# Small scales in PSUM or off VectorE, attention's scale in the softmax, and a new written order

## The chip, the cores and the metric

The kernel runs on one core of a Trainium2 chip. The metric is the device time of one execution in microseconds (us). The engines of the core are called by the names of the profile: PE (TensorE, the matrix engine; PEld are its weight loads), DVE (VectorE), ACT (ScalarE), POOL (GpSimd) and SP (SyncE, which here only issues DMAs). SBUF is the on-chip memory, PSUM the small memory in eight banks that PE writes to. PE, DVE and ACT use PSUM; POOL works in SBUF.

## The reference

Three blocks in a row on a batch of 4, a sequence of 576 and a width of 512 (8 heads of 64):

```python
scores = q @ k.T / 8                       # causal mask, and a bias
bias = -(cum[:, None] - cum[None, :])      # cum: running sum of max(s, 0)
attn = softmax(scores + minimum(bias, 0))
x = attn @ v                               # attention, B x S x 512
h = relu(x.T @ w_tok1) @ w_tok2            # mixing over the sequence
u = x + h.T
y = u + relu(u @ w_ch1) @ w_ch2            # mixing over the channels
gate = sigmoid(conv5(y, conv_w))           # 5 causal taps per channel
out = (gate * (y @ w_val)) @ w_out
```

Inputs and outputs are float32 values; the weights arrive in 8 bytes each and are decoded in the kernel.

## The kernel before

[...] Before a split the operand is divided by a power of two near its largest magnitude, so that both halves fit in float16. These powers of two, and products and reciprocals of them, are the "small scales": tensors of 128 rows and 1 to 4 columns.

A scale over all rows is made by `over_partitions` (line 531): PE turns a column into a row, DVE takes the maximum and masks it to its exponent (`band`), PE spreads the result over 128 rows by a matmul with a piece of the identity (`unit`), and DVE applies a lower bound. `Pair.scales` does it for q, k and v of a pair of heads, `su_prep` for a batch's u, `Chunk.x_scale` for a chunk's y; `Weight.scale` makes a weight's scale from sums that lie in PSUM.

The work is tiled as follows. A batch has four pairs of heads (`Pair`); a pair has five row blocks for each head (`score`, `expo`, then `p_split` or `p_turn`, then `av`). The four pairs of batch 0 are "wide": their probabilities stay in float32 and are turned by PE, not split. `norm` takes the reciprocals of the softmax sums, `x_value` multiplies attention's result by them (into `x32`), `x_split` splits `x32` into `xn`, `x_turn` turns it for the residual `R`, `tok1` and `tok2` mix over the sequence, and `tok2_out` adds to `R`. Then two chunks per batch (`Chunk`, 320 and 256 positions) run `ch1`, `ch2`, the convolution, `val` and `outp`. The attention of the next batch runs beside the chunks of the current one.

In batch 0 there is nothing to run beside: while its attention runs, the weights are loaded, decoded (`decode`: shifts and ors on DVE, conversions on ACT), scaled and split. The first matmul of `ch1` of batch 0 needs all four pairs and `su_prep`.

The order of the instructions is a written table, `ORDER`: each entry names an engine (P, V, A, G, S) and a task's number, and each engine's queue runs in that order. Where a step may run on one of several engines (`one` for first halves, `two` for second halves), the table chooses. A planner (`Plan`) walks the table with cost formulas; the only thing that its estimates decide in the program is how many filler matmuls `keep_warm` puts before a PE step that is expected to come late (line 526: `ones` by `ones` into an unused part of a bank; they keep PE's clock up and compute nothing). Buffers come from pools of fixed depth; tag `B` stands for seven PSUM banks that all steps share, and `give("B")` marks the point from which a bank may be reused.

Every instruction that the planner records has line 256 in the profile, so tiles and shapes tell the steps apart. Names there: `xm` is the bank of `over_partitions`, `xg` its masked column, `gm` a pair's three scales, `sg` their reciprocals, `sc` constants for the scores, `sums` the softmax sums, `xbank` attention's result in PSUM, `raw`, `top` and `arena` the weights, `wsg` a weight's reciprocal scale, `su` and `sx` the scales of u and y.

Of the kernel before, what the change touches and what calls it, by code (L numbers as in the profile page):

```python
# [8 lines left out]
F32 = mybir.dt.float32  # L9
# [10 lines left out]
TINY = 2.0 ** -90  # L20
# [8 lines left out]
    one=1852.52, two=84.11, two_w=-7.7, taps=1388.05, sign=123.61, fill=-32.64, value=0, copy=0,  # L29
)  # L30

COSTS = dict(
    one=dict(A=(0.833, 186), V=(0.52, 1130), G=(0.84, 310)),
# [47 lines left out]
S12 S0 V0 S7 P8 P1 A13 V1 S10 V1 P1 A13 V13 V1 A11 V13 V1 A11 V11 V11 P13 S138 P11 A3 A9 S139 S21 S18 A2 V2 A3 A9 V9  # L81
V9 A2 V2 S2 G5 G5 A141 A141 A141 S32 P9 V14 V14 A17 G17 A16 S27 S140 V3 P142 V142 V142 P142 V142 V142 V142 V143 V143
A144 V144 S191 S30 P19 A22 A22 V16 S145 V22 V22 P28 A29 A29 V29 A20 P22 S34 S145 S190 G15 V15 V29 A31 A20 V20 V20
P20 G6 G6 A33 A33 V33 V33 P33 S46 V23 V23 A31 V31 S192 S41 G6 S242 V31 A35 A35 V35 G146 P169 V169 A170 P155 V155
A156 P149 V149 A150 P153 V153 A154 P147 V147 A148 P161 P175 V175 P178 V178 P171 P31 G25 G25 P29 A193 P151 V161 V171
A151 S44 A193 S48 P157 A157 P176 A193 V176 P179 V179 G24 P157 A157 A162 P159 A172 V159 A177 A160 V26 G6 P152 P152
P194 V194 V194 V35 P194 V194 V194 V194 V196 V195 V196 V195 S197 S197 G24 P42 P157 A157 A180 P173 A173 P35 V36 V36
S58 G39 V40 G40 A43 P158 P158 P163 A163 P173 A173 P163 A163 P181 A181 P173 P163 A163 P164 P164 V165 V165 V166 G167
A43 V43 A173 A45 A45 V45 V45 P181 A181 A47 A47 V47 V43 P181 A181 P174 P174 P182 P182 S243 P45 S69 A38 V167 P168 A49
A49 V49 A49 P43 S55 A168 V47 S244 V183 V183 V184 A185 G198 P199 P201 P207 V199 P221 P213 P211 P230 V201 P227 A200  # L90
V207 A202 P203 A203 A208 V213 A214 G49 P49 S60 P205 P47 S62 V185 P187 P187 V211 A212 P215 V227 P228 V205 P186 V221
P223 G4 V230 P231 A245 S294 A187 V187 P188 V50 V231 V228 P188 P56 A245 A186 A245 P246 G39 A215 V50 V246 V188 V246
P215 V223 A206 P209 P204 P246 V246 V189 A222 G51 V246 G53 P204 V246 V248 V247 V248 V247 S249 S249 G250 G54 G37 V189
V189 A215 A209 A59 P209 A209 A224 P209 A209 P215 A215 A59 A229 P225 A232 S296 P210 P210 P216 P216 V217 V217 V218
P233 V59 V59 A225 A57 P225 A233 P233 A225 P225 A233 A225 A57 V57 V57 P233 A233 P70 A71 A71 V71 A61 G37 P226 P226
P234 P234 S295 P220 P59 G219 V219 V71 P71 S72 P257 G38 A63 A63 V63 V235 G51 P253 A61 V61 A220 V235 A236 G237 V63
V257 A258 P265 V265 A266 V253 A254 P259 V259 A260 P251 V251 A252 P279 V279 P275 V275 P273 G54 V61 P282 A297 V237
P255 V282 A255 V273 S467 P63 P261 P256 P256 A297 A261 S74 A297 P263 P61 A73 A274 G52 P280 P57 V64 P298 V298 V298 S76
A276 A73 P261 V263 A264 A261 P283 P298 V298 V298 P239 S468 V298 A299 V280 A281 G300 V300 P267 A267 P277 A277 P239
P267 V299 S301 A75 V283 V64 G66 P261 A267 A261 P262 P262 P267 G52 P238 V73 V73 P73 S78 G53 S301 A75 V75 A284 P285  # L100
S469 V75 A239 V239 A267 P268 P268 A77 A77 V77 P277 A285 P285 P240 V269 V269 V270 V271 V271 A470 P240 V240 A77 A285
A277 P277 P285 P75 A238 V241 V241 V241 A277 P278 P278 A79 A79 V79 V79 A470 G77 G302 P311 V311 P305 V305 P309 V309
# [1660 lines left out]
```

## Time and profile before

| what | us |
|---|---|
| median of 3 timed runs | 648.89 |
| lowest and highest | 648.29, 650.25 |
| profiled execution, whole time | 648.36 |
| its span, first to last instruction | 646.2 |

In the span the engines are busy: PE 94%, PEld 76%, DVE 78%, ACT 59%, POOL 38%. The page's slices of 16 us show PE at two tenths in the first slice and seven in the second, and at nine or more in most slices from the third on; DVE stands at eight or nine tenths in most slices up to the thirty-first. The granted clock of PE is nine tenths or more in every slice. PE's busy time includes the filler matmuls, so the share alone says little on the early slices; they are read with line 526 taken off.

### The profile page before, as it was taken

The numbers are of one execution on the slowest core, as the hardware profiler recorded it, in microseconds if no ns is written. First come the engines' busy times: TensorE is split into PE (matmuls) and PEld (weight loads), VectorE is DVE, ScalarE is ACT, GpSimd is POOL, SyncE is SP. The second block draws the span as 40 slices with busy tenths as digits, with TensorE's granted clock in tenths as the row PEclk, the third lists the DMA queues.
The fourth block names the chain that finished last, engine by engine and source line by source line (L and its number), as shares of the span: only waits on it lengthen the run. The fifth ranks groups of instructions, "written<-read, shape, count | busy, mean of one in ns | idle before, by whom it ended". The sixth has DMA issues, their size and how long they took to land.

```text
span 646.2 us, 15964 instructions
## 1 busy us (share of the span) xinstructions
PE 609.8 (94%) x6092; PEld 491.5 (76%) x6092; DVE 502.5 (78%) x1394; ACT 380.5 (59%) x809; POOL 244.1 (38%) x343
## 2 busy tenths in 40 slices
PE   2799899979999999999999999998999999999997
PEld 2789798866788888677787787776878877678864
DVE  6898899899898988888879968886798752535772
ACT  5597798877767794546674575436676502123343
POOL 1544657352443434441443344454333310641100
PEclk9999999999999999999999999999999999999999
DMA  8988676687754858582756394835673300000012
GB/s 224 233 203 237 146 199 180 167 194 154 170 115 96 163 96 153 98 177 61 145 87 132 64 168 88 177 72 104 102 133 62 84 1 34 1 2 1 1 50 82
DMA packets 190807, 75.19 MB, mean 116 GB/s; under 512 B 178213, under 2 KB 181381, under 8 KB 190730
## 3 DMA queue, kind: packets, MB, share of 16 engines
q1 hardware_dynamic: 190730, 74.16, 53.2%
q8 instruction: 48, 0.79, 0.5%
q14 instruction: 29, 0.24, 0.1%
HBM read 33.89 MB, written 4.83 MB: 60 GB/s over the span
## 4 chain that ended last, share of the span: by engine, by line
PE 51%; DVE 6%; DMA 4%; issue 2%; SPq 1%; POOL 1%; ACT 1%; POOLq 0%; ACTq 0%; DVEq 0%
PE c L256 28%; PE v L256 7%; PE o L256 6%; PE t L256 3%; DMA pT<-p 3%; PE S L256 3%; PE xbank L256 3%; DVE gate L256 2%; DVE x L256 1%; SPq L256 1%; POOL p L256 1%; DMA qk<-qkT 1%; DVE p L256 1%; PE xT L256 1%; DVE R L256 1%
## 5 line engine op out<-in xcount | busy, mean ns | idle before, releaser
L256 PEld LDWEIGHTS <-arena 128*128 128x128 f16 x3168 | 287.7, 98 | 69.2 <-issue 2.8
L256 PE MATMUL c<-hT,arena 128*128 128x256 f16 (+1 forms) x1152 | 158.6, 286 | 0.0
L256 PE MATMUL c<-u,arena 128*128 128x256 f16 (+1 forms) x1152 | 156.2, 286 | 1.0 <-DVE hT L256 0.7
L256 ACT ACTIVATE x<-x,st 128x448 f32<-128x448 f32 (+4 forms) x160 | 85.0, 556 | 49.6 <-DVE st L256 48.7
L256 POOL TENSOR_TENSOR p<-x,p 128x320 f16<-128x320 f32 (+4 forms) x82 | 67.6, 829 | 114.1 <-ACT p L256 71.3
L256 DVE CUSTOM_DVE_ANT_0 x<-S,mask,sc 128x192 f32<-128x192 f32 (+4 forms) x160 | 73.7, 484 | 19.4 <-PE S L256 14.6
L256 ACT ACTIVATE hT<-c 128x320 f16<-128x320 f32 (+1 forms) x96 | 37.4, 405 | 78.7 <-PE c L256 77.5
L256 DVE SCALAR_TENSOR_TENSOR hT<-c,hT 128x320 f16<-128x320 f32 (+1 forms) x96 | 41.3, 448 | 34.4 <-ACT hT L256 34.3
L256 PE MATMUL xbank<-v,pT 128*128 128x65 f16 (+1 forms) x880 | 60.8, 208 | 3.2 <-DMA pT<-p 3.2
L256 DVE SCALAR_TENSOR_TENSOR gate<-R,cwt,gate 128x320 f32<-128x320 f32 (+1 forms) x104 | 57.0, 567 | 1.1
L256 PE MATMUL v<-x,arena 128*128 128x256 f16 (+1 forms) x384 | 53.2, 286 | 0.0
L256 PE MATMUL S<-qkT 128*128 128x64 f16 (+4 forms) x192 | 49.2, 277 | 3.5 <-DVE st L256 1.1
L256 PE MATMUL S<-qk 67*128 67x64 f16 (+4 forms) x192 | 49.7, 278 | 2.9 <-DMA qk<-qkT 2.8
L256 POOL TENSOR_SCALAR p<-x 128x192 f16<-128x192 f32 (+4 forms) x44 | 20.0, 456 | 72.5 <-ACT x L256 41.1
L256 PE MATMUL o<-arena,g 128*128 128x512 f16 x192 | 45.1, 379 | 0.0
L256 PEld LDWEIGHTS <-pT 128*128 128x128 f16 x960 | 37.3, 98 | 7.7 <-DMA pT<-p 3.9
L526 PE MATMUL xbank<-ones 128*128 128x112 bf16 x485 | 36.0, 223 | 4.8 <-DVE x L256 3.5
L526 PEld LDWEIGHTS <-ones 128*128 128x128 bf16 x485 | 31.6, 106 | 5.4 <-issue 4.1
L256 ACT ACTIVATE gate<-gate 128x1280 f32<-128x1280 f32 (+1 forms) x24 | 27.9, 1161 | 8.0 <-DVE gate L256 7.5
L256 PEld LDWEIGHTS <-g 128*128 128x128 f16 x192 | 18.5, 99 | 18.1
L256 ACT ACTIVATE p<-x 128x576 f16<-128x576 f32 (+4 forms) x56 | 27.3, 490 | 6.2 <-DMA pT<-p 5.1
L256 ACT ACTIVATE top<-raw 128x512 f32<-128x512 f32 (+2 forms) x36 | 22.5, 629 | 13.8 <-DMA raw<-in_moe_w_ch_dram 5.7
(204 smaller groups left out, 1102.4 us busy)
## 6 DMA issues: line engine op xcount, KB each, us to landing
raw<-in_moe_w_ch_dram SPq DMA_DIRECT2D x24, 512.0 KB
stg<-in_q_dram SPq DMA_DIRECT2D x16, 288.0 KB
stg<-in_k_dram SPq DMA_DIRECT2D x16, 288.0 KB
qk<-qkT SPq DMA_DIRECT2D x32, 144.0 KB
out_dram<-ot SPq DMA_DIRECT2D x16, 256.0 KB
vst<-in_v_dram SPq DMA_DIRECT2D x24, 128.0 KB
raw<-in_moe_w_val_dram SPq DMA_DIRECT2D x4, 512.0 KB
raw<-in_moe_w_out_dram SPq DMA_DIRECT2D x4, 512.0 KB
```

Source lines behind the costliest of these rows:

```text
L256: return f(*a, **k)
L526: plan.idle = lambda: nc.tensor.matmul(xbank[:, 400:512], lhsT=ones, rhs=ones[:, 0:112], start=True, stop=True)
```

## The change

- `over_partitions` writes the maximum and the bounded scale into the PSUM bank instead of SBUF, and its caller reads them there; the caller gives the bank back after its last use. The factor that `su_prep` and `x_scale` applied afterwards (4 and 2^14) now lies in the matrix that spreads (`unit2`, `unit14`), so that instruction goes and a copy into SBUF comes. `Pair.scales` has seven DVE instructions behind the spreading matmul instead of five.
- `Weight.scale` keeps its intermediates in the bank of the sums.
- The product that `tok2_out` needs (`sg[:, 3:4]`), and those of `su_rest` and `so_rest`, go to ACT or POOL (`times`, cost class `tiny`); so do the three products of weights' scales (`product`, POOL).
- Attention's result is scaled in the softmax: `norm` multiplies the sums by v's scale for all pairs, so `x32` holds scaled values. `x_split` then needs no scale: the second half is a plain subtraction and may run on DVE or POOL (before: DVE only). `x_turn` multiplies the scale back on ACT while it copies from PSUM.
- The planner's cost formulas and its rule for what shares a port change, and the table `ORDER` is written anew.

Counted in the order: DVE has 1302 rows for 1316, ACT 689 for 674, POOL 348 for 327, SP 304 for 304; the filler matmuls are 452 for 485, and of the 33 fewer 40 fewer stand before the first matmul of `ch1` of batch 0 (428 for 468). Before that matmul PE has 726 other matmuls in both. Of the 32 second halves of `xn`, 32 were on DVE; now 19 are on DVE and 13 on POOL.

The first pair's scales on DVE, before (`xm_250` is the bank, `0_0` stands for batch and pair):

```order
L256 TENSOR_REDUCE xg1_83<-xm_250 3x1
L256 TENSOR_SCALAR xg1_83<-xg1_83 3x1
L256 TENSOR_TENSOR gm_0_0_238<-xm_250,floor3_95 128x3
L256 RECIPROCAL sg_0_0_239<-gm_0_0_238 128x3
L256 SCALAR_TENSOR_TENSOR sc_0_0_240<-sg_0_0_239,gck_113 128x1
L256 SCALAR_TENSOR_TENSOR sc_0_0_240<-gm_0_0_238 128x1
L256 TENSOR_SCALAR sc_0_0_240<-two24_107,sg_0_0_239 128x2
L256 TENSOR_SCALAR qk16_0_0_267<-stg_0_0_175,sg_0_0_239 128x9x64
L256 SCALAR_TENSOR_TENSOR qk16_0_0_267<-stg_0_0_175,sg_0_0_239,qk16_0_0_267 128x9x64 x2
```

and now:

```order
L257 TENSOR_REDUCE xm_262<-xm_262 3x1
L257 TENSOR_SCALAR xg1_83<-xm_262 3x1
L257 TENSOR_TENSOR xm_262<-xm_262,floor3_95 128x3
L257 RECIPROCAL xm_262<-xm_262 128x1
L257 RECIPROCAL sg_0_0_253<-xm_262 128x3
L257 COPY gm_0_0_252<-xm_262 128x2
L257 SCALAR_TENSOR_TENSOR sc_0_0_254<-xm_262,gck_112,sg_0_0_253 128x1
L257 SCALAR_TENSOR_TENSOR sc_0_0_254<-xm_262,gm_0_0_252 128x1
L257 TENSOR_SCALAR sc_0_0_254<-xm_262 128x1
L257 SCALAR_TENSOR_TENSOR qk16_0_0_276<-stg_0_0_187,sg_0_0_253,qk16_0_0_276 128x9x64 x2
```

The chain has two more instructions; the reciprocal that the splits of q and k need (`sg`) is the third behind the matmul, not the second, and what it reads lies in PSUM.

The first pair's `xn` on DVE, before, with the second half of the first three row blocks between the decoding of the weights:

```order
L256 SCALAR_TENSOR_TENSOR raw_446<-top_777,raw_446 128x512
L256 SCALAR_TENSOR_TENSOR arena_115<-top_694,raw_458 128x512
L256 SCALAR_TENSOR_TENSOR xn_129<-x32_128,sc_0_0_240,xn_129 128x384
L256 SCALAR_TENSOR_TENSOR raw_578<-top_837,raw_578 128x512
L256 SCALAR_TENSOR_TENSOR arena_115<-top_777,raw_446 128x512
L256 TENSOR_SCALAR sums_0_0_756<-xbank_81 128x4
L256 RECIPROCAL sums_0_0_756<-sums_0_0_756 128x4
L256 TENSOR_TENSOR x32_128<-xbank_81,sums_0_0_756 128x256
```

and the same place now:

```order
L257 SCALAR_TENSOR_TENSOR arena_114<-top_796,raw_426 128x512
L257 SCALAR_TENSOR_TENSOR raw_492<-top_817,raw_492 128x512
L257 SCALAR_TENSOR_TENSOR arena_114<-top_718,raw_448 128x512
L257 TENSOR_SCALAR sums_0_0_745<-xbank_81,sc_0_0_254 128x4
L257 RECIPROCAL sums_0_0_745<-sums_0_0_745 128x4
L257 TENSOR_TENSOR x32_127<-xbank_81,sums_0_0_745 128x256
```

The second half is gone from DVE. On POOL there stood before:

```order
L256 TENSOR_SCALAR arena_115<-arena_115,wsg_c10_685 128x512 x2
L256 TENSOR_TENSOR arena_115<-arena_115 128x512
L256 TENSOR_SCALAR xn_129<-x32_128,sc_0_0_240 128x384
L256 TENSOR_SCALAR qk2_0_1_456<-one16_110,sc_0_1_590 3x1152
L256 TENSOR_TENSOR arena_115<-raw_578 128x512
```

and now:

```order
L257 TENSOR_SCALAR xn_128<-x32_127 128x384
L257 TENSOR_TENSOR xn_128<-x32_127,xn_128 128x384
L257 TENSOR_SCALAR qk2_0_1_450<-one16_109,sc_0_1_586 3x1152
L257 TENSOR_TENSOR arena_114<-raw_492 128x512
L257 TENSOR_TENSOR xn_128<-x32_127,xn_128 128x256
L257 TENSOR_SCALAR arena_114<-arena_114,wsg_t2_462 128x576
L257 TENSOR_TENSOR arena_114<-arena_114 128x576
L257 TENSOR_SCALAR arena_114<-arena_114,wsg_c10_675 128x512 x2
L257 TENSOR_SCALAR sg_0_0_253<-gm_0_0_252,ru0_117 128x1
```

POOL has both halves of the first three row blocks, the second half of the other two, and, behind two splits of a weight, the product for `tok2_out` of the first pair.

The diff, without most of the cost formulas and the table, of which the first row stands for the rest:

```diff
 ORDER = """
-S12 S0 V0 S7 P8 P1 A13 V1 S10 V1 P1 A13 V13 V1 A11 V13 V1 A11 V11 V11 P13 S138 P11 A3 A9 S139 S21 S18 A2 V2 A3 A9 V9
...
-    def band(dst):
-        V.tensor_scalar(dst.bitcast(I32), dst.bitcast(I32), EXPMASK, None, ALU.bitwise_and)
+    def band(dst, src=None):
+        src = dst if src is None else src
+        V.tensor_scalar(dst.bitcast(I32), src.bitcast(I32), EXPMASK, None, ALU.bitwise_and)
...
         PE.transpose(ps[:n, 0:rows], src, ident[:rows, :rows])
+        yield V
+        V.tensor_reduce(ps[:n, 200:201], ps[:n, 0:rows], AX.X, ALU.max)
         yield V, "xg"
         g = free_xg.pop(0)
-        V.tensor_reduce(g[:n], ps[:n, 0:rows], AX.X, ALU.max)
...
-        yield V
-        band(g[:n])
+        band(g[:n], ps[:n, 200:201])
...
         yield V
-        V.tensor_tensor(dst, ps[:, 256:256 + n], floor, ALU.max)
-        give("B")
+        V.tensor_tensor(ps[:, 264:264 + n], ps[:, 256:256 + n], floor, ALU.max)
+        return ps, ps[:, 264:264 + n]
+
+    def times(dst, x, scale):
+
+        yield tiny(1)
+        if plan.engine is A:
+            A.activation(dst, x, AF.Copy, scale=scale)
+        else:
+            G.tensor_scalar(dst, x, scale, 1.0, ALU.mult, ALU.mult)
...
-            yield from over_partitions(gm[:, 0:3], self.am[:, 0:3], floor3[:, 0:3], unit=unit14)
+            ps, g = yield from over_partitions(self.am[:, 0:3], floor3[:, 0:3], unit=unit14)
             yield V
-            V.reciprocal(sg[:, 0:3], gm[:, 0:3])
+            r = ps[:, 272:273]
+            V.reciprocal(r, g[:, 0:1])
+            V.reciprocal(sg[:, 0:3], g)
+            V.tensor_copy(gm[:, 1:3], g[:, 1:3])
             yield V, "qk16"
...
-            V.scalar_tensor_tensor(sc[:, 0:1], sg[:, 0:1], gck[:, 2:3], sg[:, 1:2], ALU.mult, ALU.mult)
-            V.scalar_tensor_tensor(sc[:, 1:2], gm[:, 0:1], -0.125, gm[:, 1:2], ALU.mult, ALU.mult)
-            V.tensor_scalar(sc[:, 2:4], two24, sg[:, 2:3], None, ALU.mult)
+            V.scalar_tensor_tensor(sc[:, 0:1], r, gck[:, 2:3], sg[:, 1:2], ALU.mult, ALU.mult)
+            V.scalar_tensor_tensor(sc[:, 1:2], g[:, 0:1], -0.125, gm[:, 1:2], ALU.mult, ALU.mult)
+
+            V.tensor_scalar(sc[:, 3:4], g[:, 2:3], 2.0 ** 10, None, ALU.mult)
+            give("B")
...
-            if self.wide:
-                V.tensor_scalar(rr, total, 1e-9, None, ALU.add)
-            else:
-                V.tensor_scalar(rr, total, 1e-9, self.sc[:, 3:4], ALU.add, ALU.mult)
+
+            V.tensor_scalar(rr, total, 1e-9, self.sc[:, 3:4] if self.wide else 2.0 ** 10, ALU.add, ALU.mult)
...
-            kx = self.sc[:, 2:3]
-            scaled(xn[:, 0, t], x32[:, t], kx)
-            yield V
-            rest(xn[:, 1, t], x32[:, t], kx, xn[:, 0, t])
+            scaled(xn[:, 0, t], x32[:, t], 1.0)
+            yield two(n)
+            plan.engine.tensor_tensor(xn[:, 1, t], x32[:, t], xn[:, 0, t], ALU.subtract)
...
-            A.activation(self.Rb[:, self.hp, HALO + b0:HALO + end], ps[:, 0:end - b0], AF.Copy)
+            A.activation(self.Rb[:, self.hp, HALO + b0:HALO + end], ps[:, 0:end - b0], AF.Copy, scale=self.sc[:, 3:4])
...
-            yield V
-            V.scalar_tensor_tensor(self.sg[:, 3:4], self.gm[:, 2:3], 2.0 ** 14, ru0, ALU.mult, ALU.mult)
+            yield from times(self.sg[:, 3:4], self.gm[:, 2:3], ru0)
...
-            yield from over_partitions(t[:, 1:2], t[:, 0:1], floor1)
-            V.reciprocal(t[:, 2:3], t[:, 1:2])
-            V.tensor_scalar(t[:, 2:3], t[:, 2:3], 4.0, None, ALU.mult)
+            _, g = yield from over_partitions(t[:, 0:1], floor1, unit=unit2)
+            V.reciprocal(t[:, 2:3], g)
+            V.tensor_copy(t[:, 1:2], g)
+            give("B")
```

## Rows read from the trace of the kernel before

**Rows 1.** The page, part 1: busy us, share of the span, instructions.

```profile
span 646.2 us, 15964 instructions
...
PE 609.8 (94%) x6092; PEld 491.5 (76%) x6092; DVE 502.5 (78%) x1394; ACT 380.5 (59%) x809; POOL 244.1 (38%) x343
```

**Rows 2.** Stretch, length, busy us (instructions) of PE, PEld, DVE, ACT, POOL, PEclk, DMA, GB/s.

```profile
0.00:140.00 140.00, 114.46 (x1284) 104.52 (x1285) 120.78 (x359) 107.86 (x243) 67.17 (x95) 1.00 0.79 200
140.00:640.00 500.00, 492.71 (x4801) 386.04 (x4799) 381.74 (x1036) 271.26 (x565) 176.88 (x248) 1.00 0.47 93
```

**Rows 3.** The same stretches, line 526 (filler matmuls) alone.

```profile
0.00:140.00 140.00, 31.89 (x438) 28.55 (x439) 1.00 0.79 200
140.00:640.00 500.00, 4.10 (x51) 3.02 (x48) 1.00 0.47 93
```

**Rows 4.** Timeline near 140 us: start, us, engine, line, operation.

```profile
140.09 1.66 DVE L256 SCALAR_TENSOR_TENSOR u<-R,su,u 128x640 f16<-128x640 f32 x2
...
142.39 0.84 PE L256 MATMUL c<-u,arena 128*128 128x320 f16 x5
```

**Rows 5.** Waits of PE, 15 to 140 us: total us, times, longest.

```profile
PE xbank L526 <- DVE x L256: 3.5, 3, 1.8
PE S L256 <- DMA qk<-qkT: 2.2, 1, 2.2
PE xm L256 <- ACT junk L256: 1.4, 1, 1.4
...
PE pb L256 <- ACT pg L256: 0.4, 1, 0.4
```

**Rows 6.** DVE by shape, 0 to 140 us: count, busy us, mean ns, idle.

```profile
L256 DVE TENSOR_SCALAR qk<-stg,sg 128x576 f16<-128x576 f32 x5 | 3.9, 805 | 0.0
L256 DVE SCALAR_TENSOR_TENSOR xn<-x,sc,xn 128x384 f16<-128x384 f32 x4 | 3.8, 938 | 0.1
...
L256 DVE TENSOR_SCALAR sc<-two,sg 128x2 f32<-128x2 f32 x6 | 2.3, 390 | 0.0
...
L256 DVE SCALAR_TENSOR_TENSOR xn<-x,sc,xn 128x256 f16<-128x256 f32 x4 | 2.2, 546 | 0.0
L256 DVE SCALAR_TENSOR_TENSOR sc<-sg,gck 128x1 f32<-128x1 f32 x6 | 2.1, 348 | 0.2
...
L256 DVE SCALAR_TENSOR_TENSOR sg<-gm,ru 128x1 f32<-128x1 f32 x4 | 1.6, 409 | 0.0
L256 DVE SCALAR_TENSOR_TENSOR arena<-arena,wsg_t 128x512 f16<-128x512 f32 x1 | 1.6, 1629 | 0.0
L256 DVE TENSOR_SCALAR xn<-x,sc 128x384 f16<-128x384 f32 x2 | 1.6, 789 | 0.1
...
L256 DVE RECIPROCAL sg<-gm 128x3 f32<-128x3 f32 x6 | 1.0, 171 | 0.1
...
L256 DVE SCALAR_TENSOR_TENSOR sc<-gm 128x1 f32<-128x1 f32 x6 | 0.9, 150 | 0.0
...
L256 DVE TENSOR_TENSOR gm<-xm,floor 128x3 f32<-128x3 f32 x6 | 0.9, 149 | 0.8 <-PE xm L256 0.8
...
L256 DVE TENSOR_SCALAR sums<-xbank 128x6 f32<-128x6 f32 x4 | 0.6, 157 | 0.6 <-PE xbank L256 0.6
...
L256 DVE TENSOR_SCALAR sums<-xbank,sc 128x6 f32<-128x6 f32 x1 | 0.2, 210 | 0.0
```

**Rows 7.** DVE by shape, whole run: subtraction without a scale.

```profile
L256 DVE TENSOR_TENSOR p<-x,p 128x448 f16<-128x448 f32 x10 | 6.2, 617 | 0.1
...
L256 DVE TENSOR_TENSOR p<-x,p 128x320 f16<-128x320 f32 x4 | 2.0, 490 | 0.6 <-POOL p L256 0.5
```

**Rows 8.** POOL by shape, whole run: the same subtraction.

```profile
L256 POOL TENSOR_TENSOR p<-x,p 128x320 f16<-128x320 f32 x20 | 16.4, 819 | 20.9 <-ACT p L256 10.4 <-DVE R L256 6.3 <-ACT x L256 3.1
```

**Rows 9.** ACT by shape, whole run: 64 columns with and without a scale operand.

```profile
L256 ACT ACTIVATE x<-xbank,sums 128x64 f32<-128x64 f32 x64 | 14.5, 321 | 7.7 <-DVE sums L256 7.7
...
L256 ACT ACTIVATE p<-x 128x64 f16<-128x64 f32 x9 | 2.3, 254 | 0.2
```

More of the change, by code (lines that the diff above doesn't have):

```diff
@@ L28 @@
 SHY = dict(
-    one=1852.52, two=84.11, two_w=-7.7, taps=1388.05, sign=123.61, fill=-32.64, value=0, copy=0,
+    tiny=0, one=1852.52, two=84.11, two_w=-7.7, taps=1388.05, sign=123.61, fill=-32.64, value=0, copy=0,
 )
 COSTS = dict(
+    tiny=dict(A=(0.83, 190), G=(0.84, 300)),
     one=dict(A=(0.833, 186), V=(0.52, 1130), G=(0.84, 310)),
@@ L86 @@
[L86 to L90, printed above, removed]
@@ L336, in cost_dve @@
         n = max(cols(x) for x in a[:2] if isinstance(x, bass.AP))
-        fast = name == "tensor_scalar" and k.get("accum_out") is None
-        n += 72 * (name == "tensor_tensor_reduce")
-        return n * (0.52 if fast else 1.04) + 69 + 61 * (n > 16 and any(isinstance(x, bass.AP) and cols(x) == 1 for x in a))
+        fast = name == "tensor_scalar" and k.get("accum_out") is None and (a[0].shape[-1] >= 128 or n <= 16)
+        if name == "tensor_tensor_reduce":
+            return n * 1.04 + 144
+        return n * (0.52 if fast else 1.04) + 69 + (61 if n > 16 else 35) * any(isinstance(x, bass.AP) and cols(x) == 1 for x in a[2:])
     def cost_pool(self, name, a, k):
@@ L372, in shares @@
         if name in ("tensor_scalar", "tensor_copy"):
-            return len(inner) == len(tensors)
+            return len(inner) == len(tensors) and (n <= 16 or a[0].shape[-1] >= 128)
+        if name == "scalar_tensor_tensor":
+            inner = [x for x in (a[0], a[1], a[3]) if x.space != bass.MemoryType.PSUM]
         return name in ("scalar_tensor_tensor", "tensor_tensor", "tensor_tensor_scan") and len(inner) > 2
@@ L477, in gated_block_kernel @@
     V, A, G, PE, SY = plan.dve, plan.act, plan.pool, plan.pe, plan.sync
-    one, two, two_w, taps, signed, fillers, values, copies = (
-        lambda n, c=c: plan.any_of(n, c) for c in ("one", "two", "two_w", "taps", "sign", "fill", "value", "copy")
+    one, two, two_w, taps, signed, fillers, values, copies, tiny = (
+        lambda n, c=c: plan.any_of(n, c) for c in ("one", "two", "two_w", "taps", "sign", "fill", "value", "copy", "tiny")
     )
@@ L772, in open @@
             yield PE, "B"
-            self.ps = bank(f"ws_{self.nm}")[:, 0:self.nsum]
+            self.bank = bank(f"ws_{self.nm}")
+            self.ps = self.bank[:, 0:self.nsum]
         def dec(self, c):
@@ L1426, in so_rest @@
         def so_rest(self):
-            yield V
-            V.tensor_scalar(self.sx[:, 3:4], self.sx[:, 1:2], ro0, None, ALU.mult)
+            yield from times(self.sx[:, 3:4], self.sx[:, 1:2], ro0)
         def outp_out(self, o):
```

361 lines of the change are left out of this document (183 added, 178 removed).

## The prediction

> **What bounds the kernel now.** I read the page's busy shares first, then the table of stretches, the fillers by their line, the waits of PE, and DVE's groups by shape.
>
> The page gives PE 94% of a span of 646.2 us and DVE 78% [rows 1]. The table of stretches shows two different kernels behind that. [...] Up to 140 us PE is busy 114.46 us, but 31.89 of them are fillers [rows 2, 3]; 82.57 us are real work, and 57.4 us of the stretch are waiting or filling. So the time that can be won lies before 140 us: I call this the front. Its end is the first split of u of batch 0 on DVE at 140.09 us, and the first ch1 matmul on PE at 142.39 [rows 4]; from there on PE has work without a gap.
>
> What holds the front? DVE is busy 120.78 of the 140 us (86%), ACT 107.86 (77%), POOL 67.17 (48%), the DMA engines 0.79 [rows 2]. The waits of PE from 15 us on make eleven rows with 14.8 us in all, of which the largest, the smallest and two between stand in [rows 5]; the seven that name DVE (from x, with 3.5 us, on down) sum to 9.8 us, the two that name a DMA to 3.2, the two that name ACT to 1.8. PE's waits are short because fillers stand in the gaps, so I use only the proportion: DVE ends two thirds of them (9.8 of 14.8).
>
> **The change part by part, on DVE in the front.** Durations are those of the front [rows 6], counts are from the order up to the split of u that ends it.
>
> Halves of xn. Before: 4 x 938 + 4 x 546 ns of second halves and 2 x 789 of first halves, 7.5 us. Now three instructions are left on DVE: one second half of each width and one first half. A subtraction without a scale takes 490 ns for 320 columns and 617 for 448 [rows 7]; along that line 256 and 384 columns take 427 and 554, and I put the first half at 500 (it cannot be above the 789 of the row). Together 1.5 us: 6.0 us less.
>
> The product for tok2_out: 4 x 409 = 1.6 us less. It reads only gm and a weight's constant, both long there, so on ACT or POOL it can run ahead; POOL has it behind two splits of a weight in the first pair. Small operations there have no row; 254 ns for 64 columns on ACT [rows 9] is the nearest, and below it I would not go. It costs time only if the queue reaches it after tok2 has ended.
>
> Scales of six pairs. Behind the matmul stood 149 + 171 + 348 + 150 + 390 = 1208 ns; now seven instructions. DVE writes nothing to PSUM in the trace, so a write there is not shown. Bounds for one of the seven are the cheapest small row, 149 ns, and the dearest, 409: from 1.0 to 2.9 us a pair. Nearest are the two that read attention's result in PSUM, 157 ns without a scalar operand and 210 with one; one of the seven reads such an operand. 6 x 157 + 210 = 1.15 us: over six pairs 0.4 us less (at the ends 1.0 less or 9.9 more). Why so little is left: three of the five were cheap already, and two more are added.
>
> Norm: the eight sums of the wide pairs now read a scalar, 210 instead of 157 ns, 0.4 us more. The weights' scales keep their count, and I put them at nothing (the same bounds per instruction).
>
> The new order itself: a 512-column second half of the first weight, 1629 ns, goes from DVE to POOL, and first halves of q and k on DVE fall from 5 to 2, 3 x 805 = 2.4 us. Some six smaller exchanges of both signs I put at nothing. 4.0 us less.
>
> Sum on DVE: -6.0 - 1.6 - 0.4 + 0.4 - 4.0 = -11.6 us.
>
> What comes back. POOL gets six of the eight second halves of the front; 819 ns for 320 columns there [rows 8], 4.9 us in all, beside DVE. The rows show that DVE and POOL hold each other: DVE's second halves took 938 ns for 384 columns where the line above gives 554. [...] I let half of their 4.9 us come back to DVE as held instructions, 2.5 us, between none and all. That leaves 9.1 us less on DVE.
>
> From DVE's time to the end of the front: with two thirds of PE's waits DVE's, 6.0 us. Against it stands what is added to the chain: the splits of q and k start one small operation later (157 ns, six pairs, 0.9 us at most), ACT takes three first halves more and multiplies in x_turn, where a scale operand and another source make 321 ns of 254 [rows 9], 67 x 8 = 0.5 us. I take 1.5 us for this, all of it. The front is 4.5 us shorter.
>
> After 140 us I take nothing. Of the 7.3 us that PE idles there some may go, since DVE loses work there too, or come, since all is ordered anew: two either way. The 33 fewer fillers stand in gaps and are worth nothing by themselves. SP issues the same 304 rows, in nearly the same sequence in the front, so transfers start where they did.
>
> The sum is made against the profiled execution: 648.36 - 4.5 = 643.9. It was 0.53 us faster than the median of the three runs, 648.89, so the forecast is **644.4 us**.
>
> **The rivals.**
>
> *The front is held by something else (no change).* DVE's 9 us turn into DVE idle time, because ACT at 77% with the decoding, the loads at a DMA share of 0.79 and the hand-overs between engines set its end. For it: PE's longest single wait in the front is a DMA's, 2.2 us [rows 5], and DVE idles 19 us already. Against it: no other engine stands above 77%. Time 648 to 649. A second road leads here: small operations on PSUM dearer than the rows say, 0.1 us on each of some 65 newly reading or writing it in the front (42 in the pairs, the rest with the weights and cum), 6.5 us back on DVE, 4.3 of the end. [...] The trace does not agree: 157 ns from the bank against 171 and 150 from SBUF [rows 6].
>
> *All of it comes out.* POOL holds nothing back and DVE is the only bound: the whole 11.6 us less the chain's 1.5, so 10.1, time 638.8; with some of the 7.3 us later, down to 637. For it: the 86%. Against it: a third of PE's waits are not DVE's.
>
> *Slower: the bank is held longer.* Until now over_partitions gave its bank back right after the bounded scale, 149 ns behind the matmul. Now the pair keeps it through six more instructions, a good 1.0 us, and longer if others stand between or if the buffer for q's and k's halves is not yet free, which is waited for before the bank is given. Seven banks serve everything, and after the front PE has no spare time: 21 such chains follow there (10 pairs, 3 batches' u, 8 chunks). If PE waits 0.35 us for a bank at each, 7.4 us come on, 2.9 net of the gain: 651.8. From 0.21 us a chain the change is not faster, at 0.31 it is slower than before by 2. For it: PE idles only 7.3 us in 500, so each new wait is paid in full. Against it: that same 7.3 says that banks are not short now.
>
> **How the numbers follow.** Forecast, 3 to 6 us less (643 to 646): 0.53. No change: 0.20. All of it: 0.13. Slower: 0.14. A difference of 0.3%, 1.9 us, is what a measurement of this kernel can tell from none. Faster takes the forecast and the third case: 0.66, and a little from the second's edge makes 0.67; same 0.19; slower 0.14. The likeliest case alone spans 642 to 647. The range reaches into both outer cases, to 639.5 below and 651 above; beyond them I leave about 0.05 and 0.08.
>
> **What would show it.** Right: the first ch1 matmul on PE starts near 138 us instead of 142.4, with DVE's busy time before it near 111 us; fillers' busy time before it falls by some 3 us; the 500 us after it keep 5 to 9 us of PE idle. The small groups on the bank read 150 to 210 ns, none above 300. Held DVE instructions: the mean of qk's and the weights' second halves rises by a few per cent where POOL subtracts. Wrong: ch1 starts at 142 with DVE below 80% of the front (the first rival), or PE shows new waits after 140 us in front of scores or xm with DVE's small groups as releasers (the last). The forecast fails if the small operations on PSUM take 300 ns or more, or if ACT's waits on POOL's halves appear as PE's waits before tok1.

## The result and the profile after

The changed kernel takes 654.22 us (median of 20 runs, 649.0 to 659.9) against 648.49 (20 runs, 646.44 to 652.23). The ratio is 1.0075, with a 95% interval of 1.0052 to 1.0097: slower by 0.75%, where the forecast was 644.4, faster by 0.7%. The range, 639.5 to 651, missed it by 3 us. Ratios, here and below, leave out runs more than 1.5% above the fastest of their kernel.

The profiled execution of the changed kernel is the slowest of its runs, 659.9 us, so its losses are larger than the median's; sizes below are taken from medians and ratios, and the profile is read for places. First its page, the same lines as [rows 1], and the row of TensorE's granted clock in 40 slices, in tenths:

```profile
span 658.1 us, 15930 instructions
...
PE 617.2 (94%) x6059; PEld 498.4 (76%) x6059; DVE 488.6 (74%) x1380; ACT 384.4 (58%) x816; POOL 254.8 (39%) x367
...
PEclk9999599988999989999999999999999999999999
```

DVE did lose work, 502.5 to 488.6 us. But there is something that no row of before had: slices below nine tenths of the clock, one of them at half. The table of windows of 4 us shows where (window, its length, busy us and instructions of PE, PEld, DVE, ACT, POOL, then clock, DMA share, GB/s). First the kernel before, then the changed one:

```profile
60.00:64.00 4.00, 3.89 (x44) 3.63 (x42) 3.96 (x14) 3.91 (x11) 2.83 (x4) 1.00 0.58 118
64.00:68.00 4.00, 2.24 (x23) 2.06 (x23) 3.86 (x9) 1.92 (x5) 3.82 (x4) 1.00 0.50 95
68.00:72.00 4.00, 4.00 (x45) 3.99 (x43) 2.50 (x5) 3.96 (x8) 3.83 (x6) 1.00 0.45 93
```

```profile
60.00:64.00 4.00, 3.97 (x41) 3.64 (x39) 3.96 (x7) 4.00 (x10) 3.72 (x4) 1.00 0.07 15
64.00:68.00 4.00, 1.84 (x19) 1.64 (x18) 3.54 (x8) 1.74 (x5) 3.74 (x5) 0.88 0.77 147
68.00:72.00 4.00, 4.00 (x23) 3.94 (x22) 3.30 (x5) 4.00 (x8) 1.68 (x3) 0.50 0.33 78
72.00:76.00 4.00, 4.00 (x22) 4.00 (x20) 0.07 (x1) 0.26 (x1) 0.00 (x0) 0.50 0.16 39
76.00:80.00 4.00, 3.47 (x27) 3.08 (x27) 1.88 (x7) 1.44 (x6) 1.26 (x3) 0.50 0.38 110
80.00:84.00 4.00, 4.00 (x21) 2.50 (x20) 3.24 (x13) 3.48 (x9) 3.83 (x6) 0.50 0.92 210
```

PE idles in the same place in both, 64 to 68 us, a little longer in the changed kernel. In the changed kernel the granted clock then falls to 0.50 and stays there for 16 us, in which PE gets through 22 matmuls in 4 us instead of 45; from 72 to 76 us DVE, ACT and POOL stand nearly still. What made PE idle is in the waits of PE from 60 to 160 us (total us, times, longest):

```profile
PE xbank L530 <- DVE sums L257: 2.9, 1, 2.9
PE xbank L530 <- DVE x L257: 2.2, 1, 2.2
```

Both are waits for DVE to read the bank `xbank`, in which attention's results stand and into which the fillers write. The timeline of DVE shows the reads `sums` and `x`, and what stands ahead of them (start us, us, engine, operation):

```profile
60.98 2.79 DVE L257 SCALAR_TENSOR_TENSOR qk<-stg,sg,qk 128x576 f16<-128x576 f32 x2
63.69 0.93 DVE L257 SCALAR_TENSOR_TENSOR R<-t,sg,R 128x288 f32<-128x288 f32 x2
64.66 0.75 DVE L257 TENSOR_REDUCE amR<-R 128x1 f32<-128x576 f32 x1
65.33 0.21 DVE L257 TENSOR_SCALAR sums<-xbank,sc 128x6 f32<-128x6 f32 x1
65.58 0.19 DVE L257 RECIPROCAL sums<-sums 128x6 f32<-128x6 f32 x1
65.80 0.56 DVE L257 TENSOR_TENSOR x<-xbank,sums 128x384 f32<-128x384 f32 x1
...
143.77 1.67 DVE L257 SCALAR_TENSOR_TENSOR u<-R,su,u 128x640 f16<-128x640 f32 x2
145.36 1.54 DVE L257 SCALAR_TENSOR_TENSOR qk<-stg,sg,qk 128x576 f16<-128x576 f32 x2
146.82 0.74 DVE L257 SCALAR_TENSOR_TENSOR arena<-arena,wsgs 128x512 f16<-128x512 f32 x1
147.49 0.15 DVE L257 TENSOR_SCALAR sums<-xbank 128x6 f32<-128x6 f32 x1
```

At 64 us PE has filled the bank, and DVE reads it only behind two held second halves (2.79 us for the pair; 1.54 at 145 us) and three steps of tok2_out. (A first half is a float32 operand rounded to float16, `hi`, a second half what is left of it, `lo`; a product is the sum of hi·hi, hi·lo and lo·hi. In the kernel before, a matmul record of 65 columns of attention's product kept PE busy for 0.142 us in float32 and for 0.053 us in float16: 22.7 us for 160 records, 38.1 for 720.) At 144 us the first ch1 matmul stands in PE's row behind fillers that wait for `sums`, and `sums` stands behind u and three splits. The gap at 64 us was there before too, as PE's timeline of the kernel before shows:

```profile
67.09 0.41 PE L526 MATMUL xbank<-ones 128*128 128x112 bf16 x5 [1.76 <-DVE x L256]
```

It is 1.76 us there and 2.16 us in the changed kernel. First and last start of the ch1 matmuls, from the tile u of the changed kernel, against 142.39 in [rows 4]:

```profile
L257 PE MATMUL c<-u,arena x1152: 269/285/474, 148.1 to 609.4; 128*128 128x320 f16 x96, 128*128 128x256 f16 x96
```

So this execution's front is 5.7 us longer, and from there to the end it takes 510.0 us where the kernel before took 503.8. Two losses, and the experiments take them apart.

### The profile page after: what moved, and what is told of

Its sections match the earlier page's. It is cut to its first block, busy times and chain, and to the rows that moved or that the text cites. A ratio compares the mean times of both kernels' runs of the same rounds, so it can differ in the third digit from the quotient of the medians.

```text
span 658.1 us, 15930 instructions
## 1 busy us (share of the span) xinstructions
PE 617.2 (94%) x6059; PEld 498.4 (76%) x6059; DVE 488.6 (74%) x1380; ACT 384.4 (58%) x816; POOL 254.8 (39%) x367
## 4 chain that ended last, share of the span: by engine, by line
PE 52%; DMA 4%; DVE 1%; ACT 1%; SPq 0%; issue 0%; POOL 0%; DVEq 0%; POOLq 0%; ACTq 0%
PE c L257 29%; PE o L257 7%; PE v L257 6%; PE t L257 3%; DMA pT<-p 3%; PE S L257 3%; PE xbank L257 3%; DMA qkT<-qk 1%; PE xT L257 1%; PE xm L257 1%; SPq L257 0%; DMA qk<-qkT 0%; ACT x L257 0%; DVE x L257 0%; DVE qk L257 0%
## 5 line engine op out<-in xcount | busy, mean ns | idle before, releaser
L257 PE MATMUL c<-u,arena 128*128 128x256 f16 (+1 forms) x1152 | 158.0, 288 | 0.0
L257 POOL TENSOR_TENSOR p<-x,p 128x64 f16<-128x64 f32 (+4 forms) x83 | 68.7, 830 | 95.2 <-ACT p L257 72.1
L257 DVE CUSTOM_DVE_ANT_0 x<-S,mask,sc 128x64 f32<-128x64 f32 (+4 forms) x160 | 73.8, 485 | 25.1 <-PE S L257 13.5
L257 PE MATMUL xbank<-v,pT 128*128 128x65 f16 (+1 forms) x880 | 64.9, 213 | 4.4 <-DMA pT<-p 3.3
L257 DVE SCALAR_TENSOR_TENSOR gate<-R,cwt,gate 128x320 f32<-128x320 f32 (+1 forms) x112 | 61.1, 564 | 1.2
L257 PE MATMUL S<-qk 67*128 67x288 f16 (+4 forms) x192 | 50.4, 285 | 4.1 <-DMA qk<-qkT 4.1
L257 PE MATMUL S<-qkT 128*128 128x288 f16 (+4 forms) x192 | 50.5, 285 | 0.9 <-DVE st L257 0.9
L257 POOL TENSOR_SCALAR p<-x 128x192 f16<-128x192 f32 (+4 forms) x48 | 24.2, 505 | 61.5 <-ACT x L257 27.0
L257 DVE SCALAR_TENSOR_TENSOR qk<-stg,sg,qk 128x576 f16<-128x576 f32 x30 | 30.0, 1028 | 0.6 <-ACT qk L257 0.5
```

What stands on the lines that cost most here:

```text
L257: return f(*a, **k)
```

## The experiments

Each run was timed in several rounds beside the kernel before (medians 647.95 to 649.54 us), which every ratio refers to; "front" is everything ahead of the first ch1 matmul of batch 0, "tail" what follows. Runs that were not timed together are compared by their ratios, since the kernel before moved by 1.6 us between comparisons. Where a diff says FILLS, the fillers in front of each step of PE were fixed to those of the kernel that it comes from.

**More fillers in the changed kernel.** My first theory was that 40 fewer fillers in the front had let the clock fall.

```
-WARM_FROM, WARM_FILL, GAP1 = 12e3, 0.75, 13.87
+WARM_FROM, WARM_FILL, GAP1 = 12e3, 0.92, 13.87
```

> The changed kernel with the share of planned gaps that fillers cover raised from 0.75 to 0.92: 587 fillers instead of 452 (522 instead of 428 before the first ch1 matmul), nothing else. Theory A (the granted clock falls in the front because PE has less to do there, and that is the loss): mean clock at 0.995 or more, no stretch at 0.50 between 68 and 84 us, and a time of 646 to 649 us, which is where the line through the 20 runs of the changed kernel meets a clock of 1.00 (span 645.0, time 646.7). Theory B (the new order itself makes the work late, whatever the clock): the clock may rise, but the time stays at 652 or more, or rises by the 135 fillers. Theory C (results kept in PSUM hold their banks too long): no change, 653 to 656.

Measured: 664.65 us, ratio 1.024 (1.0191 to 1.0289), clocks of 0.974 to 0.990. Theory A missed by 16 us; B's bound held, but not its clock. The windows 60 to 80 and 80 to 100 us stand at 0.76 and 0.81: more fillers did not stop the fall, and PE's longest wait there is again that of a filler for `xbank` (2.1 us).

**Fewer fillers in the kernel before.**

```
-WARM_FROM, WARM_FILL, GAP1 = 12e3, 0.75, 13.87
+WARM_FROM, WARM_FILL, GAP1 = 12e3, 0.70, 13.87
```

> The kernel before with the share lowered from 0.75 to 0.70: 439 fillers instead of 485 (427 instead of 468 before the first ch1 matmul, which is one less than the changed kernel has), nothing else. Theory A: the granted clock falls somewhere in the front, mean 0.98 to 0.99, and the time rises to 651 to 656 and scatters by some us from run to run. Theories B and C: clock 0.999 as before, 647.5 to 649.5 us.

Measured: 646.65 us, ratio 0.9976 (0.9956 to 0.9996), clocks of 0.992 to 1.0: below what either side expected. The count of fillers was not the cause, and that part of theory A fell.

**Two moves in DVE's row.**

```
-V189 V189 V189
...
-V217 V217 V218
+V217 V217 V218 V189 V189 V189
...
-V530 A531 V531 A96 V96 A113 P111 S116 S532 P497 P497 V498
+P111 P497 P497 V498 V530 A531 V531 A96 V96 A113 S116 S532
+FILLS (those of the changed kernel)
```

> The changed kernel with the same fillers in the same places of PE's row, and two moves in the row of DVE: the sums and the product of the attention block that PE waits for at 64 to 66 us stand ahead of the three steps of tok2_out instead of behind them, and the sums that it waits for at 144.8 to 147.7 us stand ahead of three splits. Theory A: the two gaps of PE shrink from 2.2 and 2.9 us to 1.0 or less, so the clock stays at 1.00 from 68 to 84 us and 148 to 152 us; mean clock 0.993 or more, 646 to 650 us. Theory B: the moves give back at most their own two gaps, some 3 us, 650 to 652, with the clock as low as before the moves. Theory C: no change.

Measured: 647.83 us, ratio 0.9986 (0.9964 to 1.0008); against the changed kernel's 1.0075 that is 0.89%, 5.8 us, less with the same instructions and fillers. Its windows, then PE's timeline at the gap, then the ch1 matmuls:

```profile
64.00:68.00 4.00, 3.49 (x39) 3.29 (x37) 3.86 (x9) 3.46 (x8) 3.74 (x5) 1.00 0.76 145
68.00:72.00 4.00, 3.92 (x37) 3.72 (x37) 3.93 (x9) 3.36 (x6) 1.90 (x3) 1.00 0.38 84
```

```profile
64.99 0.51 PE L536 MATMUL xbank<-ones 128*128 128x112 bf16 x7 [0.51 <-DVE x L260]
```

```profile
L260 PE MATMUL c<-u,arena x1152: 269/284/317, 137.0 to 598.8; 128*128 128x320 f16 x96, 128*128 128x256 f16 x96
```

The gap is 0.51 us, the clock stays at 1.00, and ch1 starts at 137.0, earlier than before by 5.4. But its tail takes 647.4 - 137.0 = 510.4 us, and the clock falls in other places: 0.91 from 120 to 140 us, from 220 to 240 and from 340 to 360.

**The first move alone.** The diff is the upper half of the last one.

> The changed kernel with the first of the two moves alone (the read of PE's bank at 64 to 66 us ahead of tok2_out's three steps), fillers in the same places. Theory A: PE's gap there shrinks under 1 us and the clock stays at 1.00 from 68 to 84 us, so that most of the 11 us between 148.1 and 137.0 for the first ch1 matmul comes back (first ch1 at 139 to 141); the gap at 144 to 148 stays at 2.9 us with a fall of the clock behind it; 649 to 651. Rival (the clock's fall is not tied to that gap, as more fillers didn't stop it either): the clock falls between 60 and 100 us as before, 652 to 656.

Measured: 650.21 us, ratio 1.0009 (0.9994 to 1.0025). No window between 60 and 84 us is under 1.00, first ch1 at 138.4. So the late read at 65 us costs 0.66%, 4.3 us (1.0075 to 1.0009; the intervals do not meet). The second would cost 0.23%, 1.5 us, but the intervals of 1.0009 and 0.9986 overlap, so that is not shown. Its gap is still in this run: PE is busy 14.91 of the 20 us from 120 to 140, against 17.94 with both moves, and the clock stands at 0.91 there and at 0.92 from 140 to 160 us.

**The 16 waiting fillers taken out instead.** Is it the read, or the filler in front of matmuls that don't need it?

```
-FILLS step 96: 7, step 236: 9
+FILLS step 96: 0, step 236: 0
```

> The changed kernel with its own order, without the two moves, and without the 7 fillers that waited for the read of the attention bank at 66.4 us and the 9 that waited at 147.7 us; the other 436 stay. Theory H (these fillers hold up TensorE's row: the matmuls behind them need neither bank nor read): TensorE's gaps of 2.2 and 2.9 us go, the granted clock stays at 1.00 behind them, and the run comes to that of the two moves, 646.5 to 649.5. Theory A as first put (the late read itself starves TensorE, whatever stands ahead): the matmul of the attention block waits instead, the gaps stay within 0.5 us of what they were, 652 to 656.

Measured: 655.66 us, ratio 1.0085 (1.0049 to 1.0121). PE's largest waits from 60 to 160 us, then a window of 4 us:

```profile
PE c L266 <- DVE hT L266: 1.7, 1, 1.7
PE xbank L542 <- DVE x L266: 1.6, 1, 1.6
```

```profile
68.00:72.00 4.00, 4.00 (x22) 4.00 (x21) 2.89 (x5) 2.62 (x5) 1.70 (x3) 0.50 0.33 78
```

A few matmuls now run ahead, then the next filler waits for the same read, 1.6 us, and the clock falls again. Theory H as put for these 16 is wrong, and so is the second half of theory A: the matmul of the attention block is not what waits. The gap before this fall is 1.6 us, shorter than the 1.76 us of the kernel before that had no fall behind it; the length of the gap alone does not decide.

**The changed instructions in the old order.** The change's arithmetic without its order: the table of before with eight pairs of scale steps from batch 1 on some ten entries earlier, weights' scales and small products on DVE and in SBUF as before.

```
-        yield tiny(1)
+        yield V
...
+            V.tensor_reduce(pf, self.ps, AX.X, ALU.max)
...
+FILLS (those of the kernel before)
```

> The changed instructions in the order of the kernel before, with that kernel's 485 fillers in their old places: attention's scales kept in PSUM, the unscaled halves of xn and the unit matrices as in the changed kernel; the weights' scales and the small products stay on DVE and in SBUF as before; from batch 1 on, eight blocks take their two steps of scales some ten entries earlier, so that the bank is free in time. Theories A and B: the clock stays at 0.999 and the time is that of before or up to 0.4% less (645.5 to 648.5), since DVE has less to do in the front. Theory C: slower than before by 0.5% or more (652 or more), with waits of PE for the bank named xm or of PE for DVE behind it.

Measured: 645.07 us, ratio 0.9946 (0.9927 to 0.9964). This is just under the range of theories A and B; theory C is out. The instructions are a gain; the new order loses it. No PE wait for `xm` stands out (0.5 us in the tail).

**The same without the scales in PSUM.**

```
-        V.tensor_tensor(ps[:, 264:264 + n], ps[:, 256:256 + n], floor, ALU.max)
-        return ps, ps[:, 264:264 + n]
+        V.tensor_tensor(dst, ps[:, 256:256 + n], floor, ALU.max)
+        give("B")
```

> The changed instructions in exactly the order of the kernel before, with its 485 fillers, but without the part that keeps maxima and scales in PSUM: these go to SBUF as before and each bank is free at once; what is left of the change are the unscaled halves of xn and the constants in the spreading matrices. The prediction put 7.6 us of DVE's work in the front to the halves and products, and 0.4 us to the scales in PSUM, two thirds of it on the end. If that holds: within 0.2% of the run with the PSUM part (645.07 against 648.56 of before), 644.5 to 646.5. If the PSUM part carries the gain: 647.5 to 649.

Measured: 647.05 us, ratio 0.9992 (0.9969 to 1.0014), between the two answers in time; in the ratio it stands at no gain, against 0.9946 with PSUM, and the two intervals do not meet. The order here is exactly that of before, so the eight steps that the last run had earlier are back in their places too: the gain lies in the PSUM part and these eight moves together, and the halves of xn show little of it. Which of the two carries it was not tested.

**New front with the old tail, and the reverse.** The tables are cut at the first ch1 step, P351, and joined; of the two moves' run and the old-order run in the first, of the old-order run and the changed kernel in the second.

```
-ORDER = new front (two moves), new tail
+ORDER = new front (two moves), old tail
```

> The order of the run with the two moves up to the first ch1 matmul of batch 0, and behind it the order of the run that had the changed instructions in the old order; fillers of each part in their old places (445). Two steps of weights' scales come earlier, so that their bank is free. Theory A (two separate losses: the late reads of PE's bank in the front with the clock's fall behind them, and 6 to 7 us behind the first ch1 matmul that the new order costs by itself): first ch1 matmul near 137 us, 503 to 505 us from there to the end, time 642 to 645. Theory D (all loss comes from the front; the later 6 to 7 us only follow from what the front leaves late): as with the two moves, 510 us behind the first ch1 matmul, 647 to 649.

```
-ORDER = old front, old tail
+ORDER = old front, new tail
```

> The reverse: the old order with the changed instructions up to the first ch1 matmul, and the changed kernel's order behind it (492 fillers). Theory A: first ch1 matmul near 140.7 us with the clock at 0.99 or more, then 509 to 511 us, time 650 to 653, with PE's wait of 3.6 us for DVE near 90 us behind the first ch1 matmul still there. Theory D: 503 to 505 us behind it, time 644.5 to 647.

Measured: 641.35 us, ratio 0.9867 (0.9842 to 0.9892), and 653.2 us, ratio 1.0057 (1.0037 to 1.0077). First the tail of the one, then of the other, each from its first ch1 matmul to its last:

```profile
136.10:590.70 454.60, 449.47 (x4443) 354.03 (x4441) 349.57 (x984) 254.57 (x542) 176.23 (x246) 1.00 0.52 99
```

```profile
140.20:601.20 461.00, 448.35 (x4465) 354.65 (x4463) 346.99 (x960) 256.22 (x550) 175.42 (x252) 1.00 0.50 97
```

Both times lie just outside theory A's ranges, on either side. PE is busy for about the same time, but idles 5.1 and 12.7 us. In the second run the wait for the score's bank is 2.0 us instead of 3.6 in the changed kernel, and those for pT's transposes are 5.3 instead of 3.3. The new tail costs about the same behind either front, 1.19% (0.9986 against 0.9867) and 1.11% (1.0057 against 0.9946): theory D is out. The clock is not needed for this loss: in the second run's profile no slice is below nine tenths.

**One load of SP later.** Where does the new tail wait? Waits of the run with the two moves, 214 to 232 us:

```profile
PE c L260 <- DVE st L260: 3.9, 1, 3.9
DVE x L260 <- POOL p L260: 3.5, 1, 3.5
```

Its SP queue, and then POOL's row, ahead of that:

```profile
215.31 2.78 SPq L260 DMA_TRANSPOSE pT<-p  x2
218.15 2.54 SPq L260 DMA_DIRECT2D vst<-in_v_dram  x4
220.78 2.18 SPq L260 DMA_DIRECT2D vsw<-v  x2
223.07 5.06 SPq L260 DMA_TRANSPOSE pT<-p  x4
...
226.84 0.56 POOL L260 TENSOR_SCALAR p<-x 128x448 f16<-128x448 f32 x1 [1.06 <-DMA pT<-p]
227.50 0.27 POOL L260 TENSOR_SCALAR ro<-wpf 128x1 f32<-128x1 f32 x1
228.20 0.46 POOL L260 TENSOR_SCALAR p<-x 128x320 f16<-128x320 f32 x1 [0.44 <-DMA pT<-p]
228.74 0.79 POOL L260 TENSOR_TENSOR p<-x,p 128x320 f16<-128x320 f32 x1
```

Read from the end: ch2's matmul wants a bank that a score still holds; DVE's `x<-S` would free it, but wants an x buffer that POOL still reads; POOL's casts want the buffers whose transposes SP issues behind six DMAs for v. POOL's two waits for these transposes are 1.5 us, so SP's share of DVE's 3.5 us is argued from the order.

```
-S835 ... S650 ... S662 ... S656 ... S663
+S650 ... S662 ... S656 ... S663 S835
```

> The run with the two moves, and on SP one load of v (task 835, four issues) behind three transposes of p instead of ahead of them. If those loads make the transposes late, and so POOL's casts, the x buffer and the bank that PE waits 3.9 us for at 226 to 230 us: that wait falls to 2 us or less and the time to 645 to 647. If the wait only moves (PE then waits for the maximum of v's load, or the casts wait for another transpose): no change from the two moves, 647 to 649.

Measured: 649.9 us, ratio 1.0002 (0.9983 to 1.002). The wait only moved:

```profile
ACT junk L260 <- DMA vst<-in_v_dram: 5.4, 1, 5.4
PE xm L260 <- ACT junk L260: 5.1, 1, 5.1
```

The wait of 3.9 us for the score's bank is gone, and this one has come: the one move that was tried does not mend the tail.

**Fewer fillers in the best order, then none in the front.**

```
-FILLS 428 ahead of the first ch1 matmul
+FILLS 362, and in the second run 0
```

> The run with the new front (two moves) and the old tail, with 362 instead of 428 fillers before the first ch1 matmul, nothing else. Theory F (a filler that stands ready while a real matmul could go costs its place, and the clock is kept by the density of work, not by these): as taking 46 out of the kernel before gave 1.9 us, 639 to 641. Rival G (the clock is on the edge in the front, and fewer fillers let it fall): mean clock 0.99 or less, 643 to 647.

> The same with no filler at all before the first ch1 matmul (17 left behind it). Theory F and G agree here if fillers do anything: the clock falls to half in several stretches before 140 us, mean 0.96 or less, 648 to 665. If fillers are worth nothing, as the prediction had it: 636 to 641 with the clock at 0.99 or more.

Measured: 641.89 us, ratio 0.9912 (0.9881 to 0.9943), and 637.51 us, ratio 0.9835 (0.9809 to 0.986). 66 fewer show no gain (0.9912 against 0.9867, intervals that overlap). None at all gives 4.4 us against the run with 362, timed beside it (0.9835 against 0.9912, intervals apart), and the fastest kernel of the study; against the run with all 428 it is 0.32%, 2.1 us, with intervals that overlap. That is the answer for fillers that are worth nothing. Of the falls to half that both theories wanted one came, at 0.50 from 128 to 136 us and 0.76 from 136 to 140, and the mean clock is 0.992, not 0.96. Its front and tail:

```profile
0.00:131.20 131.20, 96.77 (x854) 82.26 (x854) 112.78 (x357) 106.77 (x240) 77.76 (x112) 0.99 0.81 209
131.20:586.50 455.30, 449.69 (x4440) 354.37 (x4440) 348.77 (x987) 256.40 (x544) 176.36 (x246) 0.99 0.51 100
```

**None in the front of the changed kernel, none in that of the kernel before.**

```
-FILLS 428, and in the second run 468, ahead of the first ch1 matmul
+FILLS 0
```

> The changed kernel with its own order and no filler ahead of the first ch1 matmul (24 left behind it). Theory H: the front loses its gaps and its fillers, the 6.2 us behind the first ch1 matmul stay, 642 to 647, with a mean clock of 0.985 to 0.995. Theory A as first put: the gaps stay and there is less work around them, so the clock falls more than in the changed kernel: 653 to 662.

> The kernel before without its 468 fillers ahead of the first ch1 matmul (17 left). Theory H: the three waits of fillers for VectorE go (4.7 us in all) at a clock that falls to some 0.99: 643 to 647. If fillers hold the clock in that kernel: a clock of 0.985 or less and 651 or more.

Measured: 646.37 us, ratio 0.9961 (0.9937 to 0.9986), and 642.92 us, ratio 0.9902 (0.9865 to 0.994). The first is theory H's answer; the second lies at the edge of its range, with a mean clock of 0.988 to 0.992. Without front fillers the changed kernel gains 1.14% (7.4 us), the kernel before 0.98% (5.0 us by the medians timed together), the best order the 0.3 to 0.8% above. Two windows of the changed kernel without them:

```profile
60.00:80.00 20.00, 17.47 (x146) 14.38 (x146) 19.33 (x60) 18.50 (x46) 15.18 (x18) 1.00 0.66 146
120.00:140.00 20.00, 15.61 (x128) 11.05 (x127) 18.84 (x57) 16.80 (x33) 12.34 (x16) 0.74 0.87 181
```

The fall at 68 us is gone, PE's longest gap between 60 and 140 us is 1.2 us, and another has come between 120 and 140 us, where the clock is 0.74; the first ch1 matmuls start at 133.5. From 60 to 140 us PE waits in the scale chain 2.0 us for DVE and 1.3 for ACT (1.2 the longest); whether that set the fall off is not shown, and what it costs was not measured.

## Why the prediction was wrong

**What held.** The seven instructions of a pair's scales, in the front of the run with the two moves: 166 + 173 + 180 + 128 + 214 + 148 + 148 = 1157 ns; the text had 1.15 us [rows 6]. First, second and last of them:

```profile
L260 DVE SCALAR_TENSOR_TENSOR sc<-xm,gck,sg 128x1 f32<-128x1 f32 x6 | 1.3, 214 | 0.0
...
L260 DVE TENSOR_TENSOR xm<-xm,floor 128x3 f32<-128x3 f32 x6 | 1.0, 166 | 0.7 <-PE xm L260 0.7
...
L260 DVE TENSOR_SCALAR sc<-xm 128x1 f32<-128x1 f32 x6 | 0.9, 148 | 0.0
```

The 0.1 us more for each small operation on PSUM, with which a rival reckons, stands in no run: the seven took 0.17 us each, the five before 0.24 (1208 ns). The three halves of xn left on DVE take 559 + 426 + 359 ns, 1.34 us where 1.5 stood. DVE's work ahead of the split of u falls from 120.8 to 113.2 us there: 7.6 less, where the sum had 9.1 net. With the two reads in place the first ch1 matmul starts at 137.0; the text asked for "near 138". The step from DVE's work to the end of the front came out near in size, in part by luck: 7.6 us less work gave 5.4 us where the text had 4.5 from 9.1. On how that gain divides over the parts the text was not borne out: the halves of xn without the PSUM part show next to no gain in the ratio (0.9992).

**A term too small: what comes back on DVE.** The text let 2.5 us come back, and the mean of the second halves of q and k was to rise "by a few per cent". They alone took 3.5 us more, 39%, in the front, first before, then with the two moves:

```profile
L256 DVE SCALAR_TENSOR_TENSOR qk<-stg,sg,qk 128x576 f16<-128x576 f32 x10 | 8.6, 902 | 0.0
L260 DVE SCALAR_TENSOR_TENSOR qk<-stg,sg,qk 128x576 f16<-128x576 f32 x10 | 12.1, 1252 | 0.5 <-ACT qk L260 0.5
```

Which part of the change brought this is left open. That DVE and POOL hold each other the text argued from a mean against a line; the trace of the kernel before has it instruction by instruction. Of the four second halves of xn with 384 columns in the front, two took 0.61 and 0.62 us with POOL idle (at 48.51 and 117.02 us) and two took 1.06 and 1.47 us beside POOL (71.86 and 93.30 us), so the 938 ns stand against 0.61 us, not 554 ns. But not every meeting costs: the product for tok2_out took 0.99 us at 112.40 us beside a subtraction of POOL and 0.15 us at 94.69 us beside scalings on POOL, and `sc<-gm`, which also reads SBUF alone, 0.15 us at 84.00 us beside one more.

**Step 1 that failed: "the new order itself".** I counted which instructions change engine and put "some six smaller exchanges of both signs" at nothing. That count could not show what stands ahead of a read that PE waits for. Two reads of `xbank` behind other work on DVE made gaps of a kind that [rows 5] already shows (3.5 us in three waits), and the clock fell behind them. Moving the two reads ahead, on the same engine, gave 5.8 us back.

**Step 2 that failed: "after 140 us I take nothing".** It had two us either way, of the 7.3 us that PE idles in the 500 us of [rows 2] (492.71 busy), and the new tail costs 1.19%, 7.7 us, with the same front. "Transfers start where they did" was read from SP's order in the front alone; the tail's chain runs through SP. The third rival had the place, PE waiting for a bank in a stretch with no spare time, and by chance a near time, 651.8, but not the mechanism: the bank of the longest wait was a score's, held through POOL and, as the order reads, SP, and the kernels that keep `xm` as long in the old tail lose nothing.

**Step 3 that failed: the clock.** The forecast has no term for the clock: it takes the 1.00 of [rows 2] to hold for the changed kernel too. I had no rival in which the clock falls, though [rows 2] and [rows 3] together show that 31.89 of PE's 114.46 us in the front compute nothing, and that 57.4 of the 140 us hold no real work. Whether that made the fall possible is not shown; that it came is (0.50 from 68 to 84 us).

**Step 4 that failed in part: "the 33 fewer fillers stand in gaps".** That 33 are worth nothing nearly held: 46 fewer in the kernel before gave 0.24%, 66 fewer in the best order nothing. But fillers as a whole cost time: taking all out of the front gave 1.14% and 0.98% in two orders, and 0.3 to 0.8% in the third. [rows 3] was read as filler in gaps; [rows 5] has fillers (L526) that wait for a bank themselves.

In ratios to the kernel before the loss divides so: instructions -0.54%, the new front with its reads in place -0.79, the new tail +1.19, the second late read +0.23 (not clear of noise), the first +0.66, together +0.75%, or -3.5, -5.1, +7.7, +1.5 and +4.3 us. That these sum to the whole is no proof, since each is the step from one run to the next; the tail's term alone is measured a second way, with the old front (+1.11).

Left open: why the clock fell behind a gap of 1.6 us in one run and not behind 1.76 us at the same place before; which waits make up the tail's loss, of which one chain was followed and not mended; and whether the scales in PSUM or the eight moved steps carry the gain of the instructions.

## What to carry to other kernels

When a table of order changes, go through the waits of the saturated engine one by one and look up in the new order what stands ahead of each releaser; a count of work per engine does not show it. Judge a change of instructions and a change of order by runs of their own: here -0.54% and +1.3% came as one change. Try filler work at none before tuning its amount, and look for what it waits on itself.

## What the runs showed of the hardware

- Behind 2.2 us without work at 64 us, TensorE ran at a granted clock of 0.50 for some 16 us, although it was busy 4.00 of 4 us in most of the windows there. Behind 1.76 us at the same place in the kernel before the clock stayed at 1.00, and behind 1.6 us in the run without the 16 fillers it fell to 0.50.
- A lower mean clock can go with a shorter time. The best order without front fillers has a mean clock of 0.992 and is faster by 4.4 us than its twin with 362 of them at 0.997. The runs of the kernel before without its 468 front fillers have 0.988 to 0.992, those with them, timed beside, 0.992 to 1.0, and the ratio of the two is 0.9902.
- Two second halves of q and k on DVE took 2.79 us at 61 us beside POOL, against 1.54 us at 145 us with POOL idle. POOL beside them is not enough, though: at 63.39 us in the kernel before the same two took 1.54 us beside three such instructions of POOL, which took 1.16 us each (0.69 at 138.55 us). POOL's row of the changed kernel at 61 us, then that of the kernel before at 63 us:

```profile
60.78 1.22 POOL L257 TENSOR_SCALAR qk<-one,sc 3x1152 f16<-3x1152 f16 x1
62.09 2.24 POOL L257 TENSOR_SCALAR arena<-arena,wsg_c 128x512 f16<-128x512 f32 x2
...
63.38 3.48 POOL L256 TENSOR_SCALAR arena<-arena,wsg_c 128x512 f16<-128x512 f32 x3
```

- The seven DVE instructions of a pair's scales that now read or write 1 to 3 columns in PSUM take 128 to 214 ns; those that read and write only SBUF took 150 to 409 [rows 6]. Like for like the two differ little: the reciprocal of three columns took 180 ns from the bank and 171 from SBUF.
